# First four chunks of q, k and v loaded in pairs and put in token order by matmuls, in a retention layer with a squared-ReLU FFN

## The chip, the cores and the metric

The kernel runs on one core of a Trainium2 chip. The metric is device time in microseconds, the median of ten runs. The core's engines are TensorE (PE, with its weight loads shown apart as PEld), VectorE (DVE), ScalarE (ACT), GpSimd (POOL) and SyncE (SP), which here issues all transfers. Each engine takes its own instructions in program order and waits on the others through semaphores. Sixteen DMA engines carry the transfers.

## The reference

Four sequences of 768 tokens, eight heads of 64. Each head keeps a 64x64 state that decays by a factor gamma of its own; the outputs, laid out as 3072 rows of 512, go through an FFN of width 2048 with a squared ReLU.

```python
gamma = 1.0 - 2.0 ** (-5.0 - np.arange(H))
for t in range(S):
    state = gamma[None, :, None, None] * state + np.einsum('bhd,bhe->bhde', k[:, :, t], v[:, :, t])
    y[:, :, t] = scale * np.einsum('bhd,bhde->bhe', q[:, :, t], state)
x = attn_out.transpose(0, 2, 1, 3).reshape(B * S, H * D)
h = np.maximum(x @ w_in, 0.0)
return h * h @ w_out
```

All inputs and the output are float32: q, k and v of 6 MB each, w_in and w_out of 4 MB each, the output of 6 MB.

## The kernel before, in words

**Chunks.** The 3072 tokens are 24 chunks of 128, six to a sequence. The recurrence is done in halves of 64 tokens: scores within a half, plus a state carried from half to half. The decay is folded into tables made at the start: `vf` scales v by gamma to the minus position, and `yf` (four activations on ACT, L336) scales the outputs back.

**A chunk's road.** `prepare` (L348) issues one transfer each for k, q and v from SP (L355): 128 rows (tokens), eight heads to a row, so 1024 pieces of 256 bytes and 256 KB. k and q are cast to bf16 (L343 on DVE, L341 on ACT, L345 on POOL, by the planner's choice) and v is scaled to bf16 by DVE (L366). `transpose` (L391) turns k and q: for the first NPE = 6 chunks by four 128x128 matmuls each on PE (L408) and an evacuation; for chunks 6 and 7 by 32 small matmuls of 64x64 inside a visit (`flips`, L381) and one evacuation on ACT (L387); from chunk 8 on by a DMA transpose (L399, q and k together).

A *visit* (L466) then does the matmuls of two neighbouring chunks: the outputs of chunk m (L425 from masked scores, L440 from the states) and the scores and state increments of chunk n = m + 1 (L451, L462). DVE masks the scores (L505), adds up the states (L516, L518) and writes the scaled outputs into `xt` (L527). For the first SPLIT = 6 chunks the two halves of a visit are separate pieces.

**FFN.** The output chunks go through the FFN in blocks of `BLOCKS = [1, 1, 1, 1, 1, 1, 2, 2, 2, 4, 4, 4]` chunks. FFN-1 (L565) multiplies a block by w_in, which comes in four column blocks w_in 0 to 3, each 1 MB in float32 (L541), staged in one of four buffers `wst` and cast in four pieces. ACT applies ReLU (L570) and DVE squares (L575). FFN-2 (L608) multiplies a chunk by w_out, four row blocks of 1 MB in the same staging buffers, in four quarters of four 128x512 matmuls; ACT evacuates (L616) and SP stores (L620). The last chunk is done in two column halves, each with its own evacuation and store.

**Order.** Nothing is left to a compiler. The class `Plan` places every operation by a list scheduler: each has engines it may run on, a duration, dependencies and a priority, and the engines' programs are what comes out. The constants above (durations, priorities, numbers of buffers) therefore move instructions everywhere. Transfers have priorities by the list `ORDER`. Where PE would wait before time WARM, the planner puts fill matmuls on the identity (L657). The pieces of `ORDER` name k, q, v of a chunk, and i and o for blocks of w_in and w_out:

```python
ORDER = (
    "k0 q0 q1 v0 k1 q2 v1 k2 v2 v3 k3 q3 i0 i1 q4 o0 i2 i3 k4 o1 v4 o2 o3 v5 v6 q5 k5 q6 v7 q7 k6 k7"
)
```

A block of w_out can only be issued once the block of w_in in the same staging buffer has been cast. PSUM has four banks for FFN, transposes and fills (`fps`), two for scores (`sc`) and two for outputs (`yy`).

Of the kernel before, what the change touches and what calls it, by code (L numbers as in the profile page):

```python
# [10 lines left out]
FP32 = mybir.dt.float32  # L11
BF16 = mybir.dt.bfloat16
I32 = mybir.dt.int32

AF = mybir.ActivationFunctionType
ALU = mybir.AluOpType


class Plan:
# [6 lines left out]
    DMA_LATENCY = 1.9  # L26
    LAND = 1.25
# [36 lines left out]
    def schedule(self, nbanks, max_open):  # L64
        ops = self.ops
        n = len(ops)
# [6 lines left out]
        start = [None] * n  # L73
        end = [None] * n
# [8 lines left out]
        bank_free = [0.0] * (nbanks - 1) + [WARM]  # L83
        bank_of = {}
        open_groups = set()
        pipe = 0.0
        outstanding = {e: [] for e in eng_free}
        done = 0
        issued, edge, next_fetched, history, crossed = 0, self.BLOCK0, 3.0, [], 0.0
        while done < n:  # L90
# [25 lines left out]
            if move:  # L116
                cost, n_desc, hold = dur
                out_ = outstanding[eng]
                while out_ and out_[0][0] <= t:
                    out_.pop(0)  # L120
                while sum(x[1] for x in out_) + n_desc > self.RING:
                    t = max(t, out_.pop(0)[0])
# [8 lines left out]
            if move:  # L131
                eng_free[eng] = t + hold
                pipe = max(pipe, t + self.DMA_LATENCY) + cost
                end[i] = pipe + self.LAND
                out_.append((pipe, n_desc))
                dur = hold
            else:
                if eng == "PE":
                    o["fill"] = 0
                    if t < WARM:  # L140
                        o["fill"] = int(max(0.0, t - max(eng_free[eng], 1.5) - 0.3) * FILL / 0.427)
                    issued += 2 * o["fill"]
                    todo, per = 2 * o["count"], dur / max(1, 2 * o["count"])
                    now = t
                    while issued + todo > edge:
                        step = max(0, edge - issued)
                        now = max(now + step * per, next_fetched)
                        issued, todo = max(issued, edge), todo - step
                        ahead = next((y for x, y in reversed(history) if x <= edge - self.AHEAD), 0.0)
                        ahead = max(ahead, crossed)  # L150
                        crossed = now
                        edge += self.BLOCK
                        next_fetched = ahead + min(5.7, max(0.3, pipe - ahead)) + self.FETCH
                    issued += todo
                    dur = now + todo * per - t
                    history.append((issued, t + dur))
                    o["dur"] = dur
                eng_free[eng] = t + dur
                end[i] = t + dur + o["lat"]
# [17 lines left out]
SMALL = (1.20, 65, 0.6)  # L177
TURN = (1.10, 16, 2.4)
WIDE = (2.85, 33, 0.6)
STORE = (0.80, 9, 0.6)  # L180
BLOCKS = [1, 1, 1, 1, 1, 1, 2, 2, 2, 4, 4, 4]
SPLIT = 6
AHEAD = 4
WARM = 20.0
FILL = 0.8
PACE = 8
LEAD = 2
NPE = 6
NTD = 8
QACT = 0  # L190
# [9 lines left out]
    "k0 q0 q1 v0 k1 q2 v1 k2 v2 v3 k3 q3 i0 i1 q4 o0 i2 i3 k4 o1 v4 o2 o3 v5 v6 q5 k5 q6 v7 q7 k6 k7"  # L200
# [11 lines left out]
def kernel(  # L212
# [32 lines left out]
    NLD, NBF, NQT, NXT, NH2, NWS, NOSB, NST = 4, 5, 5, 4, 3, 4, 3, 6  # L245
# [5 lines left out]
    def sb(name, shape, dt):  # L251
        return const.tile(shape, dt, name=name)
# [8 lines left out]
    pos_i = sb("pos_i", [P, S], I32)  # L261
# [5 lines left out]
    qkts = [sb(f"qkT{j}", [P, 2, NJ, P], BF16) for j in range(NQT)]  # L267
# [3 lines left out]
    h2s = [sb(f"h2{j}", [P, NFB, 512], BF16) for j in range(NH2)]  # L271
    w_in_bf = [sb(f"w_in{j}", [P, NCB, 512], BF16) for j in range(4)]
# [14 lines left out]
    def where(m):  # L287

        return divmod(m, NCH)
# [26 lines left out]

    pl.add("iota", "POOL", 0.2, (), ("ex_i",),
# [4 lines left out]
    pl.add("cmask", "POOL", 0.9, (), ("cmask",), mask, prio=-96)  # L322
    pl.add("lng", "DVE", 0.4, (), ("lng",), logs, prio=-99)
# [9 lines left out]

    def ytable():
        for p in range(NJ):
            nc.scalar.activation(yf[:, p, :], pos_i[:], AF.Exp, scale=lnt[:, p : p + 1])  # L336
    pl.add("yf", "ACT", 3.4, ("pos_i", "lnt"), ("yf",), ytable, prio=-98)

    def copy_on(eng, o, t):
        if eng == "ACT":  # L340
            nc.scalar.activation(o, t, AF.Copy)  # L341
        elif eng == "DVE":
            nc.vector.tensor_copy(o, t)  # L343
        else:
            nc.gpsimd.tensor_copy(o, t)  # L345


    def prepare(m):  # L348
        b, i = where(m)
        slot = m % NLD  # L350
        for x in "kqv":
            t = ld[x][:, slot, :]
            side = x == "q" and m < QACT
            pl.add(f"ld{x}{m}", "ACT" if side else "SP", SMALL, (), (f"ld{x}{slot}",),
                   lambda x=x, t=t, q_=nc.scalar if side else nc.sync: q_.dma_start(  # L355
                       t.rearrange("s (h d) -> s h d", h=H),
                       src[x][b, :, i * C : (i + 1) * C, :].rearrange("h s d -> s h d")),
                   prio=dma_prio[(x, m)] - 200 * side)
        for x in "kq":
            t, o = ld[x][:, slot, :], bf[x][m % NBF]  # L360
            pl.add(f"c{x}{m}", CAST[x], 0, (f"ld{x}{slot}",), (f"bf{x}{m % NBF}",),
                   lambda on, t=t, o=o: copy_on(on, o.rearrange("s j a d -> s a j d"),
                                                t.rearrange("s (a j d) -> s a j d", a=2, j=NJ)), prio=urgency(m))
        t, o = ld["v"][:, slot, :], bf["v"][m % NBF]
        pl.add(f"cv{m}", "DVE", 0.69, (f"ldv{slot}", "vf"), (f"bfv{m % NBF}",),
               lambda: nc.vector.tensor_tensor(  # L366
                   out=o[:], in0=t.rearrange("s (h d) -> s h d", h=H),
                   in1=vf[:, i, :, None].to_broadcast([P, H, D]), op=ALU.mult),
               prio=urgency(m))

    def qkeys(m):
        return [f"qkT{m % NQT}.{x}" for x in "kq"]
# [18 lines left out]
    def transpose(m):  # L391
# [3 lines left out]
        if NPE <= m < NTD:  # L395
            return
# [5 lines left out]
        for x, name in enumerate("kq"):  # L402
# [9 lines left out]
            pl.add(f"E{name}{m}", EVAC, 0, (f"gT{name}{m}",), (qkeys(m)[x],),  # L412
# [135 lines left out]
    def ffn1(blk):  # L548
# [5 lines left out]
        for f0 in range(0, NFB, per):  # L554
# [18 lines left out]
            def square(f0=f0):  # L573
# [9 lines left out]
                   prio=blk0[blk] + f0 / 16 * nb, bank=("close", grp))  # L583
# [5 lines left out]
    def ffn2(blk):  # L589
        for q4 in range(blk0[blk], blk0[blk] + blocks[blk]):  # L590
# [5 lines left out]
            for part in range(parts):  # L596
# [4 lines left out]
                for j in range(4):  # L601
                    reads = [f"h{g % NH2}.{u}.{4 * j + c}" for c in range(4)] + [f"wout{j}.{c}" for c in range(4)]

                    def mm(j=j, o1=o1, h2=h2, u=u, ns=ns, w=w):
                        ps = fps[o1["op"]["bank_index"]]
                        for c in range(4):
# [4 lines left out]
                                prio=(q4 + F2LAG) * 8 + 2 * j + 1 + part * 0.5, lat=0.2,  # L611
# [40 lines left out]
    if tc is not None:  # L652
        with tc.manual_schedule():
            for i in sequence:
                o = pl.ops[i]
                for _ in range(o.get("fill", 0)):
                    nc.tensor.matmul(fps[NBANK - 1][:], lhsT=ident[:],  # L657
                                     rhs=ident[:, None, :].to_broadcast([P, 4, P]), start=True, stop=True)
                o["fn"](o["on"]) if o["flex"] else o["fn"]()
# [31 lines left out]
```

## Time and profile before

| | |
|---|---|
| median of 10 runs | 215.91 us (215.2 to 216.72) |
| the profiled execution | 215.94 us, of which the span is 213.8 us |
| PE busy | 198.1 us, 93% of the span, 2738 matmuls |
| DVE, ACT, POOL busy | 113.3, 87.6, 40.8 us |
| FFN-1 matmuls (L565) | 93.6 us in 766 recorded |
| FFN-2 matmuls (L608) | 88.9 us in 376 recorded |
| packets | 99627, of which 92304 are under 512 bytes |
| moved | 38.15 MB, 178 GB/s in the mean |
| mean granted clock of PE | 0.967 |

How to read it: a line of the page's groups names a source line, an engine, an operation and its operands, then the busy time of the group and the mean of one. The granted clock is the share of its full rate at which TensorE may run. The chain of waits follows the work that ended last back to what released it. Matmuls overlap, so the mean of one (276 ns in L565) is longer than the step from one to the next.

### The profile page before, as it was taken

The numbers are of one execution on the slowest core, as the hardware profiler recorded it, in microseconds if no ns is written. First come the engines' busy times: TensorE is split into PE (matmuls) and PEld (weight loads), VectorE is DVE, ScalarE is ACT, GpSimd is POOL, SyncE is SP. The second block draws the span as 40 slices with busy tenths as digits, with TensorE's granted clock in tenths as the row PEclk, the third lists the DMA queues.
The fourth block names the chain that finished last, engine by engine and source line by source line (L and its number), as shares of the span: only waits on it lengthen the run. The fifth ranks groups of instructions, "written<-read, shape, count | busy, mean of one in ns | idle before, by whom it ended". The sixth has DMA issues, their size and how long they took to land.

```text
span 213.8 us, 6291 instructions
## 1 busy us (share of the span) xinstructions
PE 198.1 (93%) x2738; PEld 119.6 (56%) x2764; DVE 113.3 (53%) x249; ACT 87.6 (41%) x145; POOL 40.8 (19%) x68
## 2 busy tenths in 40 slices
PE   6574899999999999999999999999999999999992
PEld 2243799675467787766654444454444444444461
DVE  2566878665148598676755664656554433322100
ACT  8222468733235264433321744223534325534221
POOL 5322422315330123141312122231100000000000
PEclk9965699999999999999999999999999999999999
DMA  7999999999899999999999999999711010011021
GB/s 145 216 221 324 353 347 351 345 245 254 188 245 190 201 181 205 209 205 221 228 196 231 202 217 172 232 193 200 123 52 49 3 70 28 3 49 49 26 110 62
DMA packets 99627, 38.15 MB, mean 178 GB/s; under 512 B 92304, under 2 KB 92560, under 8 KB 99600
## 3 DMA queue, kind: packets, MB, share of 16 engines
q1 hardware_dynamic: 99600, 37.76, 82.4%
q8 instruction: 21, 0.34, 0.8%
q14 instruction: 6, 0.05, 0.1%
HBM read 27.26 MB, written 6.29 MB: 157 GB/s over the span
## 4 chain that ended last, share of the span: by engine, by line
PE 82%; SPq 6%; DMA 6%; issue 1%; ACT 1%; DVE 1%; POOL 0%; ACTq 0%
PE fps L565 38%; PE fps L608 37%; SPq L355 6%; DMA wst<-in_moe_w_in_dram 3%; DMA qkT<-kqs 2%; PE yy L425 2%; PE yy L440 2%; PE sc L451 1%; PE sc L462 1%; ACT osb L616 1%; ACT qkT L387 0%; PE fps L408 0%; POOL w_in L345 0%; PE yy L381 0%; DVE xt L527 0%
## 5 line engine op out<-in xcount | busy, mean ns | idle before, releaser
L565 PE MATMUL fps<-xt,w_in 128*128 128x128 bf16 (+2 forms) x766 | 93.6, 276 | 0.9 <-POOL w_in L345 0.8
L608 PE MATMUL fps<-w_out,h 128*128 128x512 bf16 (+1 forms) x376 | 88.9, 370 | 2.1 <-issue 1.1
L570 ACT ACTIVATE h<-fps 128x512 bf16<-128x512 f32 x96 | 57.3, 597 | 74.8 <-PE fps L565 74.4
L565 PEld LDWEIGHTS <-w_in 128*128 128x128 bf16 x768 | 60.7, 100 | 29.3 <-POOL w_in L345 0.9
L575 DVE TENSOR_TENSOR h<-h 128x512 bf16<-128x512 bf16 x96 | 43.2, 455 | 51.1 <-ACT h L570 50.8
L608 PEld LDWEIGHTS <-h 128*128 128x128 bf16 x400 | 37.5, 98 | 36.8
L616 ACT ACTIVATE osb<-fps 128x512 f32<-128x512 f32 (+1 forms) x25 | 14.5, 580 | 31.5 <-PE fps L608 30.4
L345 POOL CAST kqs<-kn 128x512 bf16<-128x512 f32 x24 | 15.6, 649 | 59.1 <-DMA kn<-in_k_dram 49.9
L527 DVE TENSOR_TENSOR xt<-yy,yf 128x512 bf16<-128x512 f32 x24 | 16.5, 687 | 16.0 <-PE yy L440 13.0
L345 POOL CAST kqs<-qn 128x512 bf16<-128x512 f32 x24 | 16.8, 700 | 32.1 <-DMA qn<-in_q_dram 32.1
L366 DVE TENSOR_TENSOR vs<-vn,vf 128x512 bf16<-128x512 f32 x24 | 17.0, 706 | 4.4 <-DMA vn<-in_v_dram 4.4
L505 DVE TENSOR_TENSOR pt<-sc,cmask 128x512 bf16<-128x512 f32 x24 | 16.4, 682 | 5.2 <-PE sc L462 5.2
L518 DVE TENSOR_TENSOR state<-sc,state 128x256 bf16<-128x256 f32 x40 | 16.8, 419 | 0.7
L440 PE MATMUL yy<-qkT,state 64*64 64x64 bf16 x352 | 12.2, 202 | 0.5
L408 PE MATMUL fps<-ident,kqs 128*128 128x128 bf16 x48 | 5.5, 246 | 4.6 <-POOL kqs L345 4.6
L425 PEld LDWEIGHTS <-vs 64*64 64x64 bf16 x384 | 5.2, 110 | 7.6 <-issue 7.4
L462 PE MATMUL sc<-vs,kqs 64*64 64x64 bf16 x352 | 8.0, 200 | 1.1 <-DVE vs L366 1.0
L451 PE MATMUL sc<-qkT 64*64 64x64 bf16 x384 | 7.7, 198 | 1.0 <-ACT qkT L341 0.7
L440 PEld LDWEIGHTS <-state 64*64 64x64 bf16 x352 | 7.6, 110 | 1.2 <-PE yy L440 1.2
L341 ACT ACTIVATE qkT<-fps 128x512 bf16<-128x512 bf16 x6 | 3.6, 597 | 11.2 <-PE fps L408 11.2
L425 PE MATMUL yy<-pt,vs 64*64 64x64 bf16 x384 | 7.8, 201 | 0.1
L408 PEld LDWEIGHTS <-kqs 128*128 128x128 bf16 x48 | 3.4, 108 | 8.1 <-POOL kqs L345 7.5
(32 smaller groups left out, 53.4 us busy)
## 6 DMA issues: line engine op xcount, KB each, us to landing
kn<-in_k_dram SPq DMA_DIRECT2D x24, 256.0 KB, 5.3
qn<-in_q_dram SPq DMA_DIRECT2D x24, 256.0 KB, 5.0
vn<-in_v_dram SPq DMA_DIRECT2D x24, 256.0 KB, 5.2
out_dram<-osb SPq DMA_DIRECT2D x23, 256.0 KB, 2.9
wst<-in_moe_w_in_dram SPq DMA_DIRECT2D x4, 1024.0 KB, 9.9
wst<-in_moe_w_out_dram SPq DMA_DIRECT2D x4, 1024.0 KB, 10.4
qkT<-kqs SPq DMA_TRANSPOSE x16, 5.0
out_dram<-osb SPq DMA_DIRECT2D x2, 128.0 KB, 2.1
```

The source lines that it names most:

```text
L345: nc.gpsimd.tensor_copy(o, t)
L366: lambda: nc.vector.tensor_tensor(out=o[:], in0=t.rearrange("s (h d) -> s h d", h=H), in1=vf[:, i, :, None].to_broadcast([P, H, D]), op=AL ...
L425: nc.tensor.matmul(yy[L * c : L * c + L, sub, p * L : p * L + L], lhsT=vs[r, 4 * a + j, :], rhs=pt[r, a, j, :], start=(p == 0), stop=True, ...
L440: nc.tensor.matmul(yy[L * c : L * c + L, sub, p * L : p * L + L], lhsT=st[r, j, :], rhs=qkT[r, 1, j, sub * L : sub * L + L], start=False, ...
L505: lambda: nc.vector.tensor_tensor(out=pt[:], in0=sc[:, :, 0:256].rearrange("s g (p t) -> s g p t", p=NJ), in1=cmask[:, None, None, :].to_b ...
L518: f = lambda cc=cc, j1=j1, j0=j0: nc.vector.tensor_tensor(out=sts[j1][:], in0=cc, in1=sts[j0][:], op=ALU.add)
L527: lambda: nc.vector.tensor_tensor(out=xt[:, :, u * C : u * C + C].rearrange("s p (g t) -> s g p t", g=2), in0=yy[:, :, 0:256].rearrange("s ...
L565: nc.tensor.matmul(ps[:, u * n : u * n + n], lhsT=w_in_bf[j][:, cb, c * P : (c + 1) * P], rhs=xt[:, cb, cols], start=(cb == 0), stop=(cb = ...
L570: nc.scalar.activation(h2[:, f0 : f0 + per, cols], ps[:].rearrange("p (u n) -> p u n", u=per), AF.Relu)
L575: nc.vector.tensor_mul(hv, hv, hv)
L608: nc.tensor.matmul(ps[:, 0:w], lhsT=h2[:, fb, u * C : u * C + C], rhs=w_out_bf[j][:, c, ns], start=(fb == 0), stop=(fb == NFB - 1))
L616: lambda o1=o1, slot=slot, ns=ns, w=w: nc.scalar.activation(osbs[slot][:, ns], fps[o1["op"]["bank_index"]][:, 0:w], AF.Copy),
```

## The change

q, k and v of the first four chunks come in pairs of chunks (`together`). A row of the loaded tile holds two neighbouring tokens, so that a piece is 2 x 64 float32, 512 bytes, and a transfer 512 KB in 1024 pieces. Even and odd tokens (g = 0, 1) are cast apart into `twin`. k and q are turned from there by PE, and the evacuation writes every other column of `qkT`, which restores the token order. k and v are also needed with a token to a partition: two 128x512 matmuls with a 0/1 matrix `perm` place the rows of each chunk, and ACT evacuates them. v may be scaled by DVE or POOL. The `twin` tiles and the position table share memory with the third `h2` buffer.

Ahead of all work stand 60 matmuls of 1x1. The fills become 128x256 and come only between 6.5 and 13 us of the plan. Blocks, split, priorities and the order of the loads are others: in the program of SP six pair loads and q of chunk 4 now stand ahead of w_in 0, where twelve small loads stood; the pools of cast and of turned chunks get one buffer more each (5 to 6). Chunk 6 is turned on PE as chunks 4 and 5 are; only chunk 7 by small matmuls. In FFN-2 the second half of the last chunk follows the first, where the quarters of both alternated. The planner's own cost model of transfers changes too; of it only the constants are shown.

```diff
-BLOCKS = [1, 1, 1, 1, 1, 1, 2, 2, 2, 4, 4, 4]
-SPLIT = 6
+BLOCKS = [2, 1, 1, 2, 2, 4, 4, 4, 4]
+SPLIT = 4
 AHEAD = 4
-WARM = 20.0
-FILL = 0.8
-PACE = 8
+WARM = 12.0
+FILL = 0.215
+WARMING = 5.5
+PACE = 4
 LEAD = 2
-NPE = 6
+NPE = 7
 NTD = 8
-QACT = 0
+PRE = 60
+CVT = {'DVE': 0.69, 'POOL': 1.1}
+TCAST = {'DVE': 0.43, 'ACT': 0.63, 'POOL': 0.78}
+TEVAC = {'ACT': 0.6, 'DVE': 0.62}
+MEVAC = {'ACT': 0.6}
+NPAIR = 2
...
-    "k0 q0 q1 v0 k1 q2 v1 k2 v2 v3 k3 q3 i0 i1 q4 o0 i2 i3 k4 o1 v4 o2 o3 v5 v6 q5 k5 q6 v7 q7 k6 k7"
+    "o0 q0 k0 v0 o1 k2 o2 q2 q4 v2 i0 o3 i1 i2 v4 k4 i3 k5 q5 q6 k6 v5 k7 v6 q7 v7"
...
-    NLD, NBF, NQT, NXT, NH2, NWS, NOSB, NST = 4, 5, 5, 4, 3, 4, 3, 6
+    NLD, NBF, NQT, NXT, NH2, NWS, NOSB, NST = 4, 6, 6, 4, 3, 4, 3, 6
...
+    def placing():
+
+        nc.gpsimd.memset(perm[:], 0.0)
+        for half in range(2):
+            r = slice(L * half, L * half + L)
+            nc.gpsimd.affine_select(out=perm[r], in_=perm[r], compare_op=ALU.not_equal,
+                                    fill=1.0, base=0, pattern=[[-1, 2], [1, P]], channel_multiplier=-2)
...
+    def together(n):
+
+
+        b, i = where(2 * n)
+        m, s0, w, twin = 2 * n, (2 * n) % NLD, n % 2, twins[n % 2]
...
+        for x in "kqv":
+            pl.add(f"ld{x}{m}", "SP", TWIN, (), held(x),
+                   lambda x=x: nc.sync.dma_start(
+                       rows_(x).rearrange("s (h n) -> s h n", h=H),
+                       src[x][b, :, i * C : (i + 2) * C, :].rearrange("h (s g) d -> s h (g d)", g=2)),
+                   prio=dma_prio[(x, m)])
...
+                    for j in range(NJ):
+                        nc.tensor.transpose(ps[:, j * P : j * P + P], twin[name][:, g, j * P : j * P + P], ident[:])
...
+                           on, qkt_all[:, q0 : q0 + 2, x].rearrange("p c j (t g) -> p c j t g", g=2)[:, :, :, :, g],
+                           fps[o1["op"]["bank_index"]].bitcast(BF16)[:, 0:512].rearrange("p (j c t) -> p c j t", j=NJ, c=2)),
...
+        for c in range(2):
+            r = slice(L * c, L * c + L)
+            for name in "kv":
...
+                    for g in range(2):
+                        nc.tensor.matmul(ps[:], lhsT=perm[r, g, :], rhs=twin[name][r, g, :], start=(g == 0), stop=(g == 1))
...
+                pl.add(f"M{name}{m + c}", MEVAC, 0, (f"gN{name}{m + c}",), (f"bf{name}{(m + c) % NBF}",),
+                       lambda on, o=o, o1=o1: copy_on(on, o, fps[o1["op"]["bank_index"]][:]),
+                       prio=urgency(m + c), lat=0.05, bank=("close", ("N", m + c, name)))
...
     def prepare(m):
+        if m < 2 * NPAIR:
+            if m % 2 == 0:
+                together(m // 2)
+            return
...
-                                prio=(q4 + F2LAG) * 8 + 2 * j + 1 + part * 0.5, lat=0.2,
+                                prio=(q4 + F2LAG) * 8 + 2 * j + 1 + part * 9, lat=0.2,
...
         with tc.manual_schedule():
+            one = nc.const_aps.tensor(1.0, [P, 1], BF16)
+            for _ in range(PRE):
+                nc.tensor.matmul(fps[NBANK - 1][0:1, 0:1], lhsT=one, rhs=one, start=True, stop=True)
             for i in sequence:
                 o = pl.ops[i]
                 for _ in range(o.get("fill", 0)):
-                    nc.tensor.matmul(fps[NBANK - 1][:], lhsT=ident[:],
-                                     rhs=ident[:, None, :].to_broadcast([P, 4, P]), start=True, stop=True)
+                    nc.tensor.matmul(fps[NBANK - 1][:, 0 : 2 * P], lhsT=ident[:],
+                                     rhs=ident[:, None, :].to_broadcast([P, 2, P]), start=True, stop=True)
```

## The prediction

> **What bounds it now.** The share of busy time says TensorE (PE 93%), but that is a mean over two stages. The page's slices separate them.
>
> ```profile
> PE   6574899999999999999999999999999999999992
> ...
> PEclk9965699999999999999999999999999999999999
> DMA  7999999999899999999999999999711010011021
> GB/s 145 216 221 324 353 347 351 345 245 254 188 245 190 201 181 205 209 205 221 228 196 231 202 217 172 232 193 200 123 52 49 3 70 28 3 49 49 26 110 62
> ```
>
> A slice is 5.3 us. For four slices PE has holes, its clock falls to half, and the DMA row is full. At 216 to 221 GB/s q, k and v go by in pieces of 256 bytes; the fourth to eighth slice carry 345 to 353, where most of the load is weights in pieces of 2 KB. After that PE is at nines to the end. The chain of waits, in order of time, shows where the one stage becomes the other, and the tail:
>
> ```profile
> 13.78 7.28 DMA wst<-in_moe_w_in_dram
> 21.11 0.88 POOL w_in L345
> 22.04 3.59 PE fps L565 x32
> ...
> 28.40 7.15 PE fps L565 x128
> ...
> 198.63 10.84 PE fps L608 x64
> 209.54 0.38 ACT osb L616
> 209.93 0.38 ACT osb L616
> ```
>
> The first FFN matmul stands at 22.04 because the first block of w_in landed at 21.1 and took 0.96 to cast. Its first 32 matmuls take 112 ns each, later ones 56 (7.15/128). From here I count PE's work. The windows name the clock:
>
> ```profile
> 10.00:15.00 5.00, 3.88 (x108) 2.46 (x112) 4.07 (x9) 1.79 (x3) 1.23 (x2) 0.69 1.29 219
> 15.00:20.00 5.00, 3.04 (x81) 1.93 (x74) 3.26 (x7) 0.66 (x2) 1.23 (x2) 0.50 1.02 281
> 20.00:25.00 5.00, 3.60 (x60) 3.42 (x60) 3.02 (x8) 2.15 (x4) 1.23 (x2) 0.50 1.10 355
> 25.00:30.00 5.00, 4.92 (x106) 4.57 (x105) 4.44 (x11) 2.70 (x6) 1.81 (x3) 0.95 1.10 366
> ```
>
> The columns after the length are busy time of PE, weight load, DVE, ACT and POOL, then clock, DMA share and GB/s. Clock 0.50 lasts to about 25.4, so some 1.75 us of the first 3.4 us of FFN are lost. Last, the timeline tells when loads land:
>
> ```profile
> 4.15 0.61 POOL L345 CAST kqs<-kn 128x512 bf16<-128x512 f32 x1 [1.20 <-DMA kn<-in_k_dram]
> ...
> 18.20 0.62 POOL L345 CAST kqs<-qn 128x512 bf16<-128x512 f32 x1 [0.37 <-DMA qn<-in_q_dram]
> ...
> 45.39 0.62 POOL L345 CAST w_out<-wst 128x512 bf16<-128x512 f32 x1 [3.31 <-DMA wst<-in_moe_w_out_dram]
> ```
>
> The first load lands 3.4 us after its issue at 0.74, the twelfth at 18.2, and the last block of w_out at 45.4. In between, a casting engine starts on w_in blocks 1 to 3 at 24.6, 28.3 and 31.1.
>
> **1. The loads.** A small load is 262,144 bytes at 218 GB/s (5 to 15 us), 1.20 us. Over 16 DMA engines that is 64 pieces each, 18.8 ns a piece. A weight block is 1 MB; the third and fourth land 2.8 us apart, 32 pieces of 2 KB each, 86 ns. The line through both is 9.2 ns and 0.0375 ns a byte, so a piece of 512 bytes takes 28.4 ns and a pair load 1.82 us, my estimate against 2.40 for two small ones. The ends: 2.40 if a byte costs what it costs at 256 bytes, and 1.36 at the weights' best rate (385 GB/s). The Trainium skill speaks for the lower end (DMA: Bandwidth & Descriptors, Specifications: pieces of 512 bytes or more run at line rate). But Perfetto Trace Analysis puts significant per-transfer overhead on everything below 2 KB. By line rate w_in would land 2.7 us earlier than I say. I take the line between the two rows, as no row shows 512 bytes.
>
> Ahead of w_in 0 stood twelve small loads (14.4 us). Now six pairs and q of chunk 4 stand there: 6 x 1.82 + 1.2 = 12.1. It lands 2.3 earlier, at 18.7. From it to the last block of w_out both queues carry seven more weight blocks and four small loads, which took 24.3 us (21.1 to 45.4); so the last lands near 43.0.
>
> **2. The road to the first FFN matmul.** In PE's order the visit that scores chunk 2 stands ahead of FFN block 0, and it needs v of chunk 2, now placed by matmuls. v2 lands about 15.7. DVE must first clear the chunk-1 work that came before it (state, mask, output: rows of 0.42, 0.69, 0.68), which by my walk down its queue ends at 17.7; its half of the cast takes 0.7, to 18.4. Two placings of two 128x512 matmuls at 0.22 to 0.43 each bring v2 to PSUM by 19.0 (at a full clock the first pair is there at 18.9). ACT evacuates it in 0.6 and, behind that in its queue, casts its quarter of w_in in 0.63. So the FFN starts at 20.2 to 20.7; I take 20.4, which is 1.65 before 22.04, not 2.3. The new work on the way: sixteen placing matmuls and eight evacuations of 0.6 on ACT (4.8 us, and ACT was busy 8.0 in the first 20 us). All lie in PE's and ACT's holes, except the one named. If the cover were gone, the price is one placing with its evacuation, 1.5 us.
>
> The 60 tiny matmuls come first, while PE waits for the first load (which lands at about 4.8, as it is twice as large). No row has 1x1. At the pace of the 64x64 matmuls (16 in 0.25 us) they take 1.0 us, at that of a 128x128 one (56 ns) 3.4; either way they end before 4.8, under the wait for the load, and I count nothing. They replace six 128x512 fills that took 0.427 us each and after which a fill took 0.38: the clock had come up. The Trainium skill (TensorE: Matmul & The Clock Gate, Part 1) asks for about 3.4 us of sustained activity, and its Part 4 says that transposes do not count. By that rule the new front, of tiny matmuls, transposes and few fills, is cold to 20.4 and for 3.4 us of FFN. I take it cold, as the row of before shows it (0.50 to 25.4 in spite of twelve fills). Were it warm, 1.75 us would come free, but the weights would take it back, as the next step shows.
>
> **3. From 20.4 to 54.6, in PE's new order.** Prices from the chain: FFN-1 group of 16 matmuls on one chunk 0.90, of 8 x 2 on two chunks 1.73; FFN-2 quarter 0.86; visit 0.82 (88.5 to 104 us); transposes 0.22. Two-chunk groups on w_in 0 at half clock to 23.8; visit 24.6; w_in 1 26.4; chunk 2 27.3; w_in 2 29.0; transposes, two groups and a visit 31.9; w_in 3 (landed 29.5) 33.6; 35.4; then FFN-2 among the last of chunk 3's FFN-1, each quarter needing its w_out: 43.7. Now the last w_out, cast at 44.1, is awaited: 0.4 lost. Behind it transposes of chunk 6 wait for k (0.25), then FFN-2 and two visits run to 54.6. With a warm clock PE comes to that wait 1.7 us sooner and waits it out.
>
> State at 54.6: FFN-1 of 4 chunks, FFN-2 of 3.75, outputs to chunk 5, scores to chunk 6, every transpose of the first eight chunks. Before, at 54.58: FFN-1 of 5, FFN-2 of 2.875, outputs and scores to chunk 4, and two sets of 64x64 turns of 0.38 still due. Left after that, at 3.58, 3.48 and 3.46 us a chunk in FFN-1 by block size and 3.45 in FFN-2: before 138.9, now 139.1 (+0.2). Visits: one and a half fewer, -1.2. Turns: -0.75. Together **-1.75**.
>
> **4. The long stage.** Before, 138.9 of FFN, 19 visits of 0.78 and the turns fill the stretch to 209.47, so no other stall is left to win. The visits now come 4 to 5 us sooner for chunks 8 to 10, and the DMA transposes with them; a chunk needs 5.4 us of the queue (three loads, a transpose 1.1, a store 0.8, my shares), PE takes 7.7. On SP several stand behind a store that waits for FFN-2: chunk 10's arrives about 1.5 us ahead of its need. A sixth buffer loosens this. I put 0 to 1 on it, and 0.2 in the sum.
>
> **5. The tail.** The last chunk's halves ran turn about and ended together, with two evacuations of 0.38 after the last matmul. Now the first half ends 1.7 us (16 x 0.108) sooner and its evacuation and store lie under the second: **-0.38**.
>
> **Sum**: -1.75 + 0.2 - 0.38 = -1.9. The profiled execution took 215.94, 2.1 more than its span, against a median of 215.91: **214.0**, span about 211.9.
>
> **Rivals.**
> - *Better than that* (0.15): line rate for 512 bytes. w_in lands at 16.0; then DVE's queue holds the start near 19.4, and the 0.65 of waits in step 3 vanish: 1.65 less, 212.4. For it, the rates at 2 KB; against it, the near 256-byte row.
> - *A slower front* (0.15): strided PSUM copies, placings and evacuations pile up, and the start slips by 1.8, to 22.2. Step 3 has 0.65 of waits to give back: 215.2, and no change at 22.9. For it: each hop in step 2 is a wait for the last; against: ACT and POOL were idle 12 of the first 20 us and more.
> - *Pairs no faster per byte* (0.12), the one on the other side: 2.40 each, so everything behind them lands 3.5 later than reckoned. The FFN starts at 23.2 and still waits for the last w_out, ready at 47.6: 217.5. From a pair time of 2.14 on the gain is gone. For it: the DMA row is at nines at 217 GB/s, so something other than requests limits; against: the pieces double, and 2 KB pieces run at 1.75 times the rate.
> - *Transposes or stores late in the long stage* (0.08): three stalls of 0.8, 216.3. One such wait (0.32 at 86.1) is in the trace.
> - *As summed* (0.50): 213.0 to 215.2.
>
> About 0.2%, 0.43 us, can be told from no change. Faster: 0.50 + 0.15 and half of the slow front, 0.72; same, the other half, 0.08; slower 0.20. The range reaches from line rate to most of the late cases, 212.3 to 216.7, leaving out the pairs at 2.40.
>
> **What would show it.** Pair loads landing 1.8 us apart; w_in 0 cast from 18.7; the first FFN matmul near 20.4 at half clock, with ACT's or DVE's queue ending its wait; a short PE wait for w_out near 44; one evacuation of 0.38 at the end. Pairs 2.2 us apart or a start after 22.2 would prove it wrong; so would new waits for qkT after 60 us.

## The result, and the profile after

| | before | after |
|---|---|---|
| median | 216.16 us (215.2 to 218.15, 52 runs) | 214.5 us (213.68 to 217.07, 15 runs) |
| ratio of the two, same chip | | 0.9917 [0.9897, 0.9937] |
| the profiled execution, and its span | 215.94, 213.8 | 214.68, 212.9 |
| time outside the span | 2.1 us | 1.8 us |
| PE: last matmul ends (model) | 209.89 us | 209.67 us |
| the last evacuation ends | 210.31 us | 210.09 us |
| from there to the span's end | 3.5 us | 2.8 us |
| packets under 512 bytes | 92304 | 79920 |

The change is worth 0.8%, with an interval from 0.6 to 1.0. The forecast was 214.0. The table already shows where to be careful: of the 1.26 us between the two profiled executions only 0.22 is PE's. The other 1.0 lies behind PE's last matmul. Single executions of either kernel scatter by more than a microsecond (spans of the changed kernel from 211.9 to 215.3 us), and this pair lies closer together than the medians do (1.66), so its 0.22 can't be trusted to better than half a microsecond.

The slices of the page after the change, where one slice is 5.3 us:

```profile
PE   3999999969999999999999999999999999999993
...
DMA  6999999999999999999999899799011011011022
GB/s 160 290 296 389 244 376 290 347 231 253 240 174 234 183 191 228 255 198 210 173 229 195 213 219 197 186 212 246 3 49 49 3 52 49 0 54 49 0 99 99
```

The second and third slices carry 290 and 296 GB/s where they carried 216 and 221. PE's holes there are gone: transposes and placings fill them. One PE slice in the FFN has fallen: the ninth (42.6 to 47.9 us) is at 6. This page has no clock row, and the 1.00 that the windows give for this execution is then no measurement; how fast PE ran has to be read from the matmuls.

When the pair loads land is told by the casts on POOL (start, duration, operands, and in brackets the wait before it):

```profile
5.19 0.79 POOL L392 CAST h<-qn 128x512 bf16<-128x512 f32 x1 [0.81 <-DMA qn<-in_q_dram]
6.89 0.87 POOL L392 CAST h<-kn 128x512 bf16<-128x512 f32 x1 [0.91 <-DMA kn<-in_k_dram]
10.51 0.87 POOL L392 CAST h<-kn 128x512 bf16<-128x512 f32 x1 [0.16 <-DMA kn<-in_k_dram]
12.37 0.62 POOL L392 CAST h<-qn 128x512 bf16<-128x512 f32 x1 [0.99 <-DMA qn<-in_q_dram]
...
19.37 0.86 POOL L392 CAST w_in<-wst 128x512 bf16<-128x512 f32 x1 [3.00 <-DMA wst<-in_moe_w_in_dram]
...
43.99 0.87 POOL L392 CAST w_out<-wst 128x512 bf16<-128x512 f32 x1 [1.85 <-DMA wst<-in_moe_w_out_dram]
46.39 0.62 POOL L392 CAST kqs<-qn 128x512 bf16<-128x512 f32 x1 [1.53 <-DMA qn<-in_q_dram]
```

DVE starts on the first pair at 5.09 and POOL on the fifth at 12.37: four loads in 7.28 us, **1.82 us each**, which is 288 GB/s. w_in 0 follows at 19.37 (21.1 before), the last block of w_out at 43.99 (45.39 before), and q of chunk 6 at 46.39.

PE's timeline shows what became of it:

```profile
20.47 3.56 PE L680 MATMUL fps<-xt,w_in 128*128 128x256 bf16 x16
...
40.60 3.62 PE L724 MATMUL fps<-w_out,h 128*128 128x512 bf16 x16
44.91 1.02 PE L724 MATMUL fps<-w_out,h 128*128 128x512 bf16 x4 [0.70 <-POOL w_out L392]
47.07 0.40 PE L523 MATMUL fps<-ident,kqs 128*128 128x128 bf16 x4 [1.13 <-POOL kqs L392]
...
56.57 1.91 PE L680 MATMUL fps<-xt,w_in 128*128 128x256 bf16 x16
```

The FFN starts at 20.47, forecast 20.4. Its first 16 matmuls of 256 columns take 223 ns each (3.56/16; the later group at 56.57 takes 119), so the clock is at half there. Up to 44.2 PE is within 0.5 us of my walk. Then it waits twice, 0.70 for the last block of w_out and 1.13 for q of chunk 6. The group at 56.57 is the state that my walk reached at 54.6; below it is called the checkpoint.

### The profile page after: what moved, and what is told of

It reads as the page before. It is cut to its first block, busy times and chain, and to the rows that moved or that the text cites. A ratio compares the mean times of both kernels' runs of the same rounds, so it can differ in the third digit from the quotient of the medians.

```text
span 212.9 us, 6020 instructions
## 1 busy us (share of the span) xinstructions
PE 200.6 (94%) x2593; PEld 112.7 (53%) x2617; DVE 116.2 (55%) x257; ACT 90.3 (42%) x151; POOL 43.6 (20%) x70
## 2 busy tenths in 40 slices
DMA packets 93386, 38.13 MB, mean 179 GB/s; under 512 B 79920, under 2 KB 86320, under 8 KB 93360
## 4 chain that ended last, share of the span: by engine, by line
PE 80%; DMA 11%; DVE 2%; ACT 2%; issue 1%; POOL 1%; SPq 0%; ACTq 0%
PE fps L724 35%; PE fps L680 34%; DMA qn<-in_q_dram 6%; DMA wst<-in_moe_w_out_dram 5%; PE yy L540 3%; PE yy L555 2%; PE fps L449 2%; PE sc L566 1%; PE sc L577 1%; PE fps L430 1%; POOL h L418 1%; DVE qkT L390 1%; DVE xt L642 1%; ACT qkT L502 0%; ACT osb L732 0%
## 5 line engine op out<-in xcount | busy, mean ns | idle before, releaser
L680 PE MATMUL fps<-xt,w_in 128*128 128x512 bf16 (+2 forms) x573 | 91.6, 312 | 0.2
L680 PEld LDWEIGHTS <-w_in 128*128 128x128 bf16 x576 | 51.5, 99 | 34.0 <-issue 0.4
L690 DVE TENSOR_TENSOR h<-h 128x512 bf16<-128x512 bf16 x96 | 41.6, 447 | 47.5 <-ACT h L685 47.2
L642 DVE TENSOR_TENSOR xt<-yy,yf 128x512 bf16<-128x512 f32 x24 | 16.5, 687 | 20.4 <-PE yy L555 18.2
L392 POOL CAST kqs<-kn 128x512 bf16<-128x512 f32 x20 | 13.3, 666 | 61.6 <-DMA kn<-in_k_dram 52.4
L392 POOL CAST kqs<-qn 128x512 bf16<-128x512 f32 x20 | 14.2, 708 | 17.8 <-DMA qn<-in_q_dram 17.8
L481 DVE TENSOR_TENSOR vs<-vn,vf 128x512 bf16<-128x512 f32 x20 | 14.1, 709 | 1.1 <-DMA vn<-in_v_dram 1.1
L390 DVE COPY qkT<-fps 128x512 bf16<-128x512 bf16 x8 | 4.6, 577 | 5.5 <-PE fps L523 2.9
L430 PE MATMUL fps<-ident,h 128*128 128x128 bf16 x32 | 4.4, 307 | 3.3 <-DVE h L390 3.2
L566 PEld LDWEIGHTS <-qkT 64*64 64x64 bf16 x384 | 5.7, 113 | 1.0 <-issue 1.0
```

Source lines behind the costliest of these rows:

```text
L566: nc.tensor.matmul(sc[cs, a, j * L : j * L + L], lhsT=qkT[r, 0, j, cs], rhs=qkT[r, 1, j, cs], start=(j == 0), stop=True, skip_group_check= ...
L642: lambda: nc.vector.tensor_tensor(out=xt[:, :, u * C : u * C + C].rearrange("s p (g t) -> s g p t", g=2), in0=yy[:, :, 0:256].rearrange("s ...
L680: nc.tensor.matmul(ps[:, u * n : u * n + n], lhsT=w_in_bf[j][:, cb, c * P : (c + 1) * P], rhs=xt[:, cb, cols], start=(cb == 0), stop=(cb = ...
L690: nc.vector.tensor_mul(hv, hv, hv)
```

## The experiments

Each ratio is against the kernel before, on the same chip, with its 95% interval. Kernels of one group that ran on one chip are also compared with each other by their medians.

**1. The changed kernel again, and without pairs.** The first is the change itself, unedited.

> The changed kernel once more, beside the others on one chip. Theory (the loads of the first 47 us set the early end, the rest of the kernel is full): 1.5 to 2.0 us under before. In the trace the first FFN matmul at 20.4 to 20.7, pair loads 1.8 us apart, PE waiting 1.5 to 2.0 us in all for the last block of w_out and for q of chunk 6.

214.59 us, ratio 0.9951 [0.9915, 0.9987]: 1.3 us under the kernel before on that chip (215.87), a little less than expected. The profiled execution took 216.8 us. Its pair loads are again 1.82 us apart (casts start at 5.21 for the first, 12.50 for the fifth), and it waited 1.94 us in all for the last w_out block and for q of chunk 6. But its front was warm, where that of the first profile was cold:

```profile
19.88 1.98 PE L680 MATMUL fps<-xt,w_in 128*128 128x256 bf16 x16 [0.26 <-POOL w_in L392]
```

The second loads and turns the first four chunks one by one, as all later ones, in about the order of the change.

```diff
-NPAIR = 2
+NPAIR = 0
-    "o0 q0 k0 v0 o1 k2 o2 q2 q4 v2 i0 o3 i1 ..."
+    "o0 q0 q1 k0 k1 v0 v1 o1 k2 k3 o2 q2 q3 q4 v2 v3 i0 o3 i1 ..."
```

> The changed kernel with the first four chunks loaded singly in 256-byte pieces, in the same order, turned as before and not placed by matmuls; all else kept. Theory (the transfers are the bound up to the last block of w_out): six pairs at 1.82 become twelve loads at 1.20, so w_in and w_out land 3.6 us later; the last w_out is cast near 48 instead of 44.9, and the time is 2.5 to 3.6 us above the changed kernel, that is 1 to 2 us above before. Rival (the placings and evacuations cost about what the pairs save): the front without them is quicker, at most 1 us above the changed kernel.

218.81 us, ratio 1.0132 [1.0094, 1.0169]. The casts on POOL:

```profile
23.52 0.87 POOL L392 CAST w_in<-wst 128x512 bf16<-128x512 f32 x1 [5.06 <-DMA wst<-in_moe_w_in_dram]
...
48.86 0.87 POOL L392 CAST w_out<-wst 128x512 bf16<-128x512 f32 x1 [2.17 <-DMA wst<-in_moe_w_out_dram]
```

With the pairs taken out, both stand over 4 us later than in the changed kernel (19.37, 43.99), and the time is 4.2 us longer (218.81 - 214.59), more than the 2.5 to 3.6 expected. The rival (at most 1 us) is out. So the pairs carry the gain, and more than the gain: everything else in the change, as the planner arranges it without pairs, costs some 2.9 us (218.81 against 215.87 for the kernel before on that chip). Of it 2.4 us are seen in w_in 0, which lands at 23.5 where it landed at 21.1; q of chunk 4 now stands ahead of it too. The rest is not taken apart.

**2. The tiny matmuls and the cold front.** The first kernel leaves the 60 matmuls out. The second replaces eight of them by 128x512 fills to wake the clock early. The order of all else on PE is that of the changed kernel.

```diff
-            for _ in range(PRE):
-                nc.tensor.matmul(fps[NBANK - 1][0:1, 0:1], lhsT=one, rhs=one, start=True, stop=True)
```

> The changed kernel without the 60 tiny matmuls, the order of everything else kept. Theory (they end at 2.4 us, under the wait for the first load, and warm nothing): the same within 0.3 us, first FFN matmul at 20.5 and 0.22 us per 256-column matmul there. Rival (they move the points at which PE's instructions are fetched, and a fetch holds up a transfer): a shift of 0.5 to 1.5 us in the landing of single loads, either way, and the time with it.

```diff
-            for _ in range(PRE):
+            for _ in range(PRE - 8):
...
+            for _ in range(8):
+                nc.tensor.matmul(fps[NBANK - 1][:], lhsT=cold[:, 0:P], rhs=cold[:], start=True, stop=True)
```

> Eight of the 60 tiny matmuls are replaced by eight of 128x512 (half clock: 0.43 us each), which end near 5.5 us; nothing else is changed. My prediction's theory (the clock in the front costs nothing, since w_in and w_out set the pace of the FFN until the last w_out block): FFN matmuls of 0.11 us from the first one on, first FFN matmul 19.4 to 20.0 us, longer waits for w_in and w_out, time within 0.3 us of the changed kernel. Rival (the 1.75 us that the 16 matmuls at half clock lose are on the path): 1.2 to 1.8 us faster, about 213 us.

Without them 214.38 us, ratio 0.9917 [0.9885, 0.9948]; with fills 214.67, 0.9933 [0.9904, 0.9962]. Both are the changed kernel's time: the 60 matmuls do nothing that can be measured. The clock did not go where I wanted it. In the kernel *without* the tiny matmuls it was up when the FFN began (16 matmuls of 256 columns in 1.92 us, 120 ns each):

```profile
18.73 0.32 PE L566 MATMUL sc<-qkT 64*64 64x64 bf16 x16
...
19.50 1.92 PE L680 MATMUL fps<-xt,w_in 128*128 128x256 bf16 x16
...
23.00 2.81 PE L680 MATMUL fps<-xt,w_in 128*128 128x256 bf16 x32 [0.68 <-POOL w_in L392]
```

In the one *with* the fills it was up early and then gone again when the FFN began (columns: window, its length, busy PE, PEld, DVE, ACT and POOL, granted clock, DMA share, GB/s):

```profile
10.00:14.00 4.00, 3.31 (x76) 1.81 (x75) 2.82 (x6) 2.85 (x6) 2.54 (x4) 1.00 1.24 269
14.00:18.00 4.00, 1.94 (x72) 1.51 (x73) 3.95 (x8) 1.30 (x3) 1.45 (x2) 1.00 1.08 373
18.00:22.00 4.00, 3.02 (x45) 1.83 (x45) 2.53 (x5) 1.60 (x3) 1.08 (x2) 0.64 1.05 384
22.00:26.00 4.00, 3.92 (x78) 2.70 (x77) 2.73 (x6) 1.71 (x3) 1.48 (x2) 0.51 0.99 213
```

PE is busy 1.94 of the 4 us ahead of the FFN, and the clock falls. So the second kernel tested nothing: its FFN ran as cold (20.27, 16 matmuls in 3.60) as the changed kernel's. The first one is the test, by luck. Its 16 matmuls are 1.6 us faster and begin a microsecond sooner, and it then waits 0.68 for w_in at 23.00 and 0.98 for w_out at 45.46. Its span is 212.6 us, that of the cold kernels 212.6 and 212.9. The kernel of experiment 6, with the same program on PE, drew a warm front too (the first line) and waits 2.04 us for w_out:

```profile
19.95 1.99 PE L680 MATMUL fps<-xt,w_in 128*128 128x256 bf16 x16 [0.43 <-POOL w_in L392]
...
46.27 1.02 PE L724 MATMUL fps<-w_out,h 128*128 128x512 bf16 x4 [2.04 <-POOL w_out L392]
```

Its span is 212.9. With the same work done, these two warm executions reach the checkpoint at 56.25 and 56.66 us, the two cold ones at 56.57 (the changed kernel) and 56.25 (with the fills). The second profile of the changed kernel, warm as well, is there only at 58.72; its clock fell again at 48, as told at the end. **A warm front is given back to the weights**, as the prediction had it.

**3. The tail.** Once put back in the changed kernel, once put alone into the kernel before.

```diff
-    prio=(q4 + F2LAG) * 8 + 2 * j + 1 + part * 9, lat=0.2,
+    prio=(q4 + F2LAG) * 8 + 2 * j + 1 + part * 0.5, lat=0.2,
```

> The changed kernel with the quarters of the two halves of the last chunk taken in turn again, as before. The prediction's step: 0.38 us more, one evacuation more after the last matmul. What the two traces suggest instead: in the kernel before the first half already ended 0.43 us ahead of the second, so the evacuation was hidden, and what is gained lies in the store, with one store of 128 KB in flight at the end and not two: 0.5 to 0.7 us more. Rival (nothing in the tail, the 0.7 is scatter of the end of the span): under 0.2.

> The kernel before with the changed kernel's tail alone: in FFN-2 the second half of the last chunk follows the first. My prediction (step 5): 0.38 us faster than before, since one evacuation less follows the last matmul. Rival A (the first half's evacuation was hidden before as well, as the trace of before shows its end ahead of the last matmul's): within 0.15 us. Rival B (the 3.9 us between PE's last matmul and the end of the span in the trace of before, against 3.2 to 3.35 in all changed kernels, come from the old order): 0.5 to 0.7 us faster, and 3.3 us behind PE's end. If 3.9 us are seen again, the tail is not the cause of that difference.

Changed kernel with the old tail: 214.65 us, 0.9933 [0.9908, 0.9959]. Kernel before with the new tail: 216.43, 0.9997 [0.9971, 1.0024]. No gain from the order of the halves can be told on either side; the interval of the second, some 0.5 to 0.6 us to each side, would by itself still allow 0.38. The traces settle it: from the end of PE's last matmul to the end of the last evacuation it is 0.42 us in both of these kernels, in the kernel before and in the changed one, so one evacuation follows the last matmul in each. The waits of SP's queue in the last microseconds, of the kernel before with the new tail:

```profile
SPq L686 <- DMA out_dram<-osb: 1.9, 1, 1.9
```

and of the changed kernel:

```profile
SPq L805 <- DMA out_dram<-osb: 1.4, 1, 1.4
```

With the new tail the kernel before still waits 1.9 us for its last store, and 3.4 us lie between its last evacuation (211.21 + 0.38) and its span's end, 215.0. So what the changed kernel saves behind PE is not the tail that was changed.

**4. Is the stretch to 47 us bound by the queue?** One kernel adds a load of 256 KB ahead of w_in 0 that nothing reads; another takes work out of the queue, with q of chunks 4 and 5 as a fifth pair.

```diff
+    pl.add("extra", "SP", SMALL, (), ("osb2.0", "osb2.1"),
+           lambda: nc.sync.dma_start(osbs[2].rearrange("s (h d) -> s h d", h=H),
+                                     q[B - 1, :, S - C : S, :].rearrange("h s d -> s h d")),
+           prio=dma_prio[("q", 4)] + 0.5)
```

> The changed kernel with one more load of 256 KB on SP's queue ahead of v of the second pair and w_in 0; nothing reads it. Theory A (the queue of loads sets the time until about 47 us): every later block lands 1.2 us later, and the time is 1.0 to 1.4 us longer than the changed kernel's, about 215.8 us. Theory B (PE's own work sets the time in the FFN's first 30 us and the waits are slack that other waits cover): at most 0.3 us longer.

215.64 us, 0.9987 [0.9966, 1.0008]; 1.0 us more than the kernel with the fills (214.67), which differs from the changed one in its first 5 us alone and ran on the same chip. Its PE line:

```profile
46.36 1.02 PE L731 MATMUL fps<-w_out,h 128*128 128x512 bf16 x4 [0.98 <-POOL w_out L394]
47.76 0.40 PE L530 MATMUL fps<-ident,kqs 128*128 128x128 bf16 x4 [0.38 <-POOL kqs L394]
```

One load more and the quarter on the last w_out block comes at 46.36 for 44.91. The queue bounds this stretch, as theory A has it, with the time at the lower end of the range given.

```diff
+    def qpair(m):
...
+               lambda: nc.sync.dma_start(
+                   rows_.rearrange("s (h n) -> s h n", h=H),
+                   q[b, :, i * C : (i + 2) * C, :].rearrange("h (s g) d -> s h (g d)", g=2)),
...
-    "... q2 q4 v2 i0 o3 i1 i2 v4 k4 i3 k5 q5 q6 ..."
+    "... q2 v2 i0 q4 o3 i1 i2 v4 k4 i3 k5 q6 ..."
```

> The changed kernel with a fifth pair: q of chunks 4 and 5 is loaded as one transfer in 512-byte pieces too, turned by four transposes a half and put in order by the eviction, so that no placing matmuls are added. Two loads of 1.2 us become one of 1.82 us. Theory A (the queue bounds the time until the last w_out block): the last w_out block lands 0.5 to 0.6 us earlier, and the time is 0.4 to 0.8 us shorter, about 214.0 us. Theory B (the wait only moves to q of chunk 6 or to PE's own work): within 0.3 us. Theory C (q of chunk 5 comes with q of chunk 4 and holds its buffer early, so that w_in blocks come later): 0.3 us or more longer.

214.47 us, 0.9934 [0.9901, 0.9966]: no gain that can be told, as theory B has it. SP now issued q of chunk 6 ahead of the last w_out block, which landed at 45.39 instead of 43.99, later and not earlier. PE waited 1.61 us for it, then none for q, and stood at the checkpoint at 55.45, with 14 quarters of FFN-2 done where the changed kernel has 15: 1.12 us sooner, 0.86 of it in work not done.

**5. The two waits behind 44 us.** First the wait for q of chunk 6, by turning chunk 6 inside its visit again.

```diff
-NPE = 7
+NPE = 6
```

> The changed kernel with one number put back: chunk 6 is turned with the 64-row form inside its visit, as before, and not by whole transposes on PE that stand in the FFN's stream and wait for q of chunk 6. Theory A (the 1.1 us that PE waited for kqs at 47.07 us is a cost of its own, behind the wait for the last w_out block): 0.3 to 1.0 us faster than the changed kernel, about 213.9 us, the wait for kqs near 47 us gone from the chain. Theory B (the queue as a whole is late, so that the next transpose or the next visit waits as long for q or v of chunk 6): within 0.2 us of the changed kernel, with a wait of about 1 us a few us later. Theory C (the 64-row form costs PE more than the wait): 0.3 us slower or more.

215.59 us, 0.9985 [0.9967, 1.0003], a microsecond *slower* than the changed kernel. The wait did go: this kernel reaches the checkpoint at 55.99, 0.58 sooner and with 16 quarters of FFN-2 for 15, 1.4 ahead in all. The time is what theory C gave, but not for its reason: this kernel loses its lead and more in the long stage, by the PE timeline:

```profile
69.59 0.32 PE L566 MATMUL sc<-qkT 64*64 64x64 bf16 x16 [0.29 <-DMA qkT<-kqs]
81.45 0.32 PE L566 MATMUL sc<-qkT 64*64 64x64 bf16 x16 [0.60 <-DMA qkT<-kqs]
90.47 7.94 PE L680 MATMUL fps<-xt,w_in 128*128 128x512 bf16 x35 [0.84 <-DVE xt L642]
```

None of these three waits is in the changed kernel. The planner rearranged everything behind the edit, so the rest of the program is not the same; the test shows the place of the wait, and that its price can't be read from the total. Next the wait for w_out: two open groups of FFN-2 are the planner's limit, three let a quarter of chunk 2 go ahead.

```diff
-    sequence = pl.schedule(NBANK, 2)
+    sequence = pl.schedule(NBANK, 3)
```

> The changed kernel with three groups of FFN-2 open at a time in the planner where two were allowed, so that a quarter of chunk 2 on w_out 0 stands ahead of the first quarter that needs the last w_out block. Theory A (the 0.7 us wait for w_out is a lack of placed work, not of work): that wait falls to 0 to 0.2 us, the wait for q of chunk 6 behind it stays at about 1 us, and the time is 0.5 to 0.8 us shorter than the changed kernel's, about 213.9 us. Theory B (q of chunk 6 is awaited all the longer): the wait for it grows to 1.8 us and the time stays within 0.3 us.

214.96 us, 0.9940 [0.9918, 0.9962]. Neither theory holds. In this execution the last w_out block landed at 45.81, and the wait grew:

```profile
46.74 1.02 PE L724 MATMUL fps<-w_out,h 128*128 128x512 bf16 x4 [1.19 <-POOL w_out L392]
47.60 0.39 PE L523 MATMUL fps<-ident,kqs 128*128 128x128 bf16 x4
```

The queue carried 207 GB/s from 35 to 40 us (275 in the changed kernel); why, these runs do not show. The quarter moved ahead did its work, as the transpose behind needs no wait, but what one execution's landing takes can be more than one quarter covers. The last kernel therefore takes three steps at once. The planner held a small load for 0.93 us, where the traces show 1.20: in its plan the last w_out block landed at 41.97, q of chunk 6 at 42.90, and the checkpoint came at 53.1.

```diff
-SMALL = (1.20, 0.93, 65, 0.6)
+SMALL = (1.20, 1.20, 65, 0.6)
...
-    sequence = pl.schedule(NBANK, 2)
+    sequence = pl.schedule(NBANK, 3)
```

and q of chunks 4 and 5 as a pair, as above.

> Three edits on the changed kernel: q of chunks 4 and 5 as a pair, three open groups of FFN-2, and the planner's price of a small load raised from 0.93 us to the 1.20 us that the traces show, so that it no longer places work ahead of its data. Theory A (the 1.8 us of waits behind 44 us are the planner's wrong price and its limit, not the queue itself): at most 0.5 us of waits for w_out and kqs between 40 and 50 us, the two-chunk FFN-1 group behind the sixth visit at 54 to 54.8 us with four whole chunks of FFN-2 done ahead of it (changed kernel: 56.57 us with three and three quarters), and 1.5 to 2.5 us faster than the changed kernel, 212.0 to 213.0 us. Theory B (the long stage after 60 us, its loads and DMA transposes, sets the end): the lead at 54 us is lost again to waits for qkT or xt, and the time is within 0.5 us of the changed kernel's.

214.2 us, 0.9902 [0.9867, 0.9938]: the lowest median of all, but not to be told from the changed kernel's. Its PE timeline:

```profile
43.78 4.71 PE L765 MATMUL fps<-w_out,h 128*128 128x512 bf16 x20
48.33 0.39 PE L564 MATMUL fps<-ident,kqs 128*128 128x128 bf16 x4
...
55.75 1.91 PE L721 MATMUL fps<-xt,w_in 128*128 128x256 bf16 x16
...
89.00 7.94 PE L721 MATMUL fps<-xt,w_in 128*128 128x512 bf16 x36 [0.84 <-DVE xt L683]
```

From 40.7 to 54.6 no wait is left over 0.2 us, so the waits were a matter of what the planner placed, as theory A has it; which of the three edits did it, this run does not separate. Theory A's time (212.0 to 213.0) did not come: the total is theory B's, within 0.5 us of the changed kernel's. The checkpoint comes at 55.75 with a whole quarter more of FFN-2 done, 1.7 us ahead in all (0.82 + 0.86), against an expected 2.6 to 3.4. It lost 1.16 at 23.7 and 0.81 at 19.1 in the front, and 0.84 of the lead goes at 89.00 to a wait for xt. PE ends at 208.85, 0.8 sooner.

**6. What was saved behind PE.** Before, the trace has seven packets on the queue that fetches code (q14), the last two at 211.37 and, behind the span, 215.68 us; after, six, the last at about 190. SP issues 115 transfers after the change, six fewer than before, and in the kernel without pairs, which issues 121 again, there are seven packets and 2.1 us outside the span. So six transfers of 256 bytes were added where the DMA engines are idle.

```diff
+            if 14 <= q4 < 20:
+                pl.add(f"pad{q4}", "SP", (0.05, 0.05, 1, 0.6), keys, (),
+                       lambda q4=q4: nc.sync.dma_start(wst[0][0:1, 0, D * (q4 - 14) : D * (q4 - 13)], q[0, 0, q4 : q4 + 1, :]),
+                       prio=0)
```

> The changed kernel with six more transfers of 256 bytes on SP, one behind each of the stores of chunks 14 to 19 (from about 150 to 193 us), where the DMA engines are nearly idle; nothing reads them, PE's program is unchanged, and SP issues 121 transfers as before the change instead of 115. Theory A (six transfers fewer make SP's program shorter, so that the fetch of its code that fell in the last microseconds before, at 205 to 215 us, and the one that followed it, no longer come; that gave 0.3 us behind the span and up to 0.6 us between the last evacuation and the span's end): one more packet on the instruction queue q14 in all (7 for 6), the last at 205 us or later, the time outside the span back at 2.1 us, and 0.3 to 1.0 us slower than the changed kernel, with PE's end unchanged. Theory B (the two have nothing to do with SP's program): time within 0.2 us of the changed kernel, outside the span 1.75 us.

214.75 us, 0.9910 [0.9888, 0.9933]: theory A's 0.3 to 1.0 us did not come. There were still six packets, the last at about 190, so the late fetch did not come back, and this run does not test what it does. What did change is the time outside the span: from 1.75 (median of the changed kernel's twelve executions) to 1.98, against 2.1 for the kernel before, which is some two thirds of the 0.3 us. The number of transfers is not all of it, since the kernel before itself has 1.7 to 1.8 in 13 of 95 executions.

The 0.7 us between the last evacuation and the end of the span are another matter. In the fourteen traces the long ending (3.4 to 3.5 us, for 2.7 to 2.9) is found only in the two kernels with the old body, and these two are also the only ones where a code fetch falls into the last store. DMA traffic from 210 to 215 us, one figure to 0.125 us, before:

```profile
GB/s 0 0 0 0 0 0 172 344 360 164 254 319 344 140 0 0 16 25 25 0 0 0 0 0 0 0 0 0 0 0 0 0 0 0 0 0 0 0 0 0
...
q14 instruction: 1, 0.01, 0.9%
```

and after, where no packet of q14 falls there:

```profile
GB/s 0 0 0 0 0 0 0 66 344 352 262 25 0 0 0 0 0 0 0 0 0 0 0 0 0 0 0 0 0 0 0 0 0 0 0 0 0 0 0 0
```

Before, the fetch (one packet of 8 KB) takes 0.70 us from 211.37. The store's other data are through at 211.8; its last eight packets of 1 KB begin at 212.07, the moment the fetch ends. So the data are all there 2.10 us behind the last evacuation. In the kernel before with the new tail the fetch takes 0.64 us from 212.68, the last eight packets begin at 213.32, and it is 2.07. In the other twelve traces no fetch falls there and it is 1.37 to 1.48. In the kernel without pairs the fetch comes at 205.6, clear of the last store, and the ending is short (2.7). The 0.7 us are thus the length of the fetch. This rests on the agreement of these times, as no run moved the fetch; what puts it there in the old body stays open.

## Why the prediction was right, and where it was not

Faster was right, the time was 0.5 us off (214.0 for 214.5), and the mechanism that carries it, pair loads in less time that bring the weights sooner, is the one I named. That the sum behind it came so near is luck. Its terms, by the two profiled executions:

- **Step 1, the pair load.** 1.82 us estimated from a line through the pieces of 256 bytes and 2 KB, 1.82 measured. The rule of line rate from 512 bytes on (the Trainium skill, DMA: Bandwidth & Descriptors, Specifications) would have made it 1.36, by my estimate with the weights' best rate of 385 GB/s. The measurement decides: 288 GB/s, between 218 and 385. "Pairs no faster per byte" was priced at 217.5; with no pairs at all, which is not quite that case, the kernel took 218.8. w_in 0 came 0.65 later than said (19.34 by the first cast, for 18.7), the last w_out block 1.0 later (43.96, for 43.0).
- **Step 2, the road to the FFN.** Right to 0.1 us (20.47), with a cold clock, in this execution; that the clock was cold in it is luck, as the second profile of the same kernel has a warm front and starts at 19.88. That tiny matmuls and clock cost nothing was right as well. The rule that I used for the cold front (the Trainium skill, TensorE: Matmul & The Clock Gate, Parts 1 and 4) fits the first execution, and not the second, nor the one without tiny matmuls, whose FFN started at full speed behind the same transposes and placings.
- **Step 3, the walk to 54.6: here it failed.** "0.4 lost" for the last w_out and "0.25" for k of chunk 6 were 0.70 and 1.13, and PE came 0.5 later to the first of them. The state of 54.6 was reached at 56.5. Instead of -1.75 against before, this step gave +0.15. (Some 0.2 of the 1.75 was a miscount: before, FFN-2 stood at 2.94 chunks at 54.58, not 2.875.) The term that I mis-sized is what lands at the end of the weights: w_out 1.0 later than said, and q of chunk 6 (not k) another 2.4 us behind it. The kernel with one load more shows that the queue is the bound there. In the planner's own plan q landed at 42.90, 3.5 us ahead of the trace, and PE's work was placed by that; with the price corrected, a third open group and a fifth pair the waits were gone.
- **Step 4, the long stage.** +0.2 was said; from the checkpoint to PE's last matmul it is about -0.4 (-0.22 at the end, less +0.15). The wait of 0.3 for qkT in the trace of before is gone, and so are 0.2 of short stops. I had counted that stage of before as without stall.
- **Step 5, the tail.** -0.38 was wrong: both experiments give nothing. Before, the first half also ended ahead of the last matmul, and its evacuation (209.54) was over when the second could start (209.93).
- **Not foreseen at all:** 0.7 us less between PE's end and the span's end, where before a code fetch lies in the last store, and 0.3 us less outside the span. Together they make up for half of the 1.9 that step 3 lost, and step 4 for some of the rest. The forecast was near because an overestimated gain and an unforeseen one partly cancel.

## What to carry to other kernels

Doubling a DMA piece from 256 to 512 bytes paid 24% of the transfer here, and to know that beforehand a line through two measured sizes was better than a threshold. When a list scheduler writes the program, compare its planned landing times with the trace: a price 0.27 us too low per small load, with five such loads between w_in 0 and q of chunk 6, makes 1.35 of the 3.5 us by which that q missed the plan, and PE waited for it. Take one edit of such a kernel as a new program, and read its effect at a checkpoint of work done, not at the total alone. Profile an unchanged kernel twice before a state such as a cold clock goes into an argument.

## What the runs showed of the hardware that was not expected

**Half clock behind two short waits.** In the second profile of the changed kernel (216.8 us, span 215.0) PE waited 0.96 and 0.98 us at 44.6 and 46.6, and the windows show what followed (columns as above):

```profile
40.00:48.00 8.00, 6.06 (x46) 3.21 (x45) 3.86 (x9) 2.94 (x5) 2.36 (x3) 1.00 1.05 286
48.00:49.00 1.00, 0.78 (x4) 0.38 (x3) 0.42 (x1) 0.00 (x0) 0.62 (x1) 0.54 0.92 202
49.00:51.00 2.00, 2.00 (x8) 0.93 (x8) 1.11 (x2) 0.60 (x1) 0.62 (x1) 0.50 1.07 233
51.00:52.00 1.00, 1.00 (x48) 0.43 (x48) 0.00 (x0) 0.00 (x0) 0.00 (x0) 0.75 1.15 218
52.00:60.00 8.00, 7.57 (x158) 4.50 (x147) 4.81 (x9) 1.83 (x3) 1.85 (x3) 1.00 1.04 252
```

Half clock for some 3 us; four matmuls of FFN-2 took 1.89 us there instead of 1.03. With waits of 0.70 and 1.13 in the same place the first profile has no such dip: its quarters there take 1.02 and 1.03. Nor has the kernel of experiment 6 behind a wait of 2.04, or the one with the fifth pair behind 1.61. So the length of the waits does not explain the dip, and its cause stays open.

**Whether the front is warm differs between executions of the same program**: the FFN's first 16 matmuls took 3.56 us in one profile of the changed kernel and 1.98 in the other. They took 1.92 in the kernel without tiny matmuls, 1.99 in the one with six transfers more, 3.60 in the one with fills.

**A code fetch can stand in the way of a store.** One packet of 8 KB on q14, 0.64 and 0.70 us long, held the last eight packets of the last store until its end in the two traces where it fell there.

**The time outside the span differs between programs in the median**: 2.1 us for 121 transfers on SP, 1.75 for 115, and 1.98 when six tiny ones are put back.
